# Attention beside a gated MLP on one core: head sums in four batches of five units, and the gate products moved from GpSimd to VectorE

## The chip, the cores and the metric

One core of one Trainium2 chip. The metric is device time of the whole program in microseconds (us), the median of several executions; lower is better. The unit of work on TensorE in this kernel is one 128x512 matmul, which takes 0.216 us here (groups of five start 1.079 us apart).

## The reference

A layer norm of x (2048 rows of 640), then two branches and a residual: attention with 32 heads of 20, where each row sees itself and the seven rows 2, 4, ... 14 before it; and a gated MLP of width 1536.

```python
def _A_ref(x, wqkv, wo):                       # H = 32, Dh = 20, W = 8, dil = 2
    q, k, v = ...                              # from x @ wqkv
    idx = pos[:, None] - (jnp.arange(W) * dil)[None, :]
    logits = jnp.einsum("bhsd,bhswd->bhsw", q, k[idx]) * Dh ** -0.5      # masked where idx < 0
    attn = softmax(logits)
    return jnp.einsum("bhsw,bhswd->bhsd", attn, v[idx]) @ wo

def _B_ref(x, w_gate, w_up, w_down):
    return ((x @ w_gate) * (x @ w_up)) @ w_down

xn = _layernorm(x)
return x + _A_ref(xn, A_wqkv, A_wo) + _B_ref(xn, B_w_gate, B_w_up, B_w_down)
```

## The kernel before

The rows are cut into four blocks of 512 (`j`), the 640 columns into five chunks of 128 (`c`). A small scheduler written in the kernel takes tasks as they become ready *by its own estimate of time* and writes down, once and for all, the order of instructions of each engine, the PSUM bank of every result, and the semaphores. (PSUM is the kernel's tile `PS`: every matmul row of the trace writes it. The kernel uses it as eight banks, and its scheduler gives a bank out again when the engine that reads the result is done with it. SBUF holds the kernel's other tiles.) So the order is fixed when the kernel is built; at run time an engine only waits.

Attention's weighted values are made in 20 units `u = 5 j + c`. VectorE multiplies values by weights (two instructions per unit), GpSimd adds pairs (two per unit, into a buffer `SV`), and TensorE sums the rest by a matmul against a quarter-width matrix `SEL`, four of which run side by side in four column groups (from the end of the wide work before to the next start, 8, 12 and 20 of them took 0.64, 0.85 and 1.29 us in the kernel before: 0.21 to 0.22 us more for each further four). This is the **narrow form**; gate, up and down use the whole width. Units are collected into batches:

```python
    NU = NJ * NCH
    BATCH = (1, 4, 6, 9, 11, 14, 19)          # last unit of each batch
    ...
        if u in BATCH:
            K.spawn(sums(tuple(pend)))
            pend.clear()

    def sums(us):
        ...
        def go(*bs):                           # one PSUM bank per unit
            for u, b in zip(us, bs):
                for dq in range(4):
                    o, p = PS[32 * dq:32 * dq + 32, b, :], SV[sv_of[u]][:, dq, :]
                    op("pe", ... e.matmul(o, SEL[:], p, start=True, stop=True, tile_position=(0, 32 * dq)) ...)
                sv_free.append(sv_of[u])

        def ev():                              # ScalarE empties the banks into OT
            ...
        yield Task("pe", go, r=[SV[sv_of[u]][:] for u in us], prio=9.7, banks=len(us), slack=0.7)
        yield Task("act", ev, r=[PS[:, b, :] for b in hold], prio=3)
```

The gate result is copied out of PSUM by ScalarE (`h`); the product with the up result is done by VectorE straight from PSUM, or, for up to `HP_MAX` at a time, by ScalarE (copy) and GpSimd (product):

```python
                def mul():
                    X = op("dve", lambda e: e.tensor_tensor(h, h, PS[:, hold[1], :], ALU.mult), ...)
                    K.free_bank(hold[1], X)    # the bank is free when VectorE is done
                ...
                if on_pool(j, m):
                    ...
                    yield Task("act", uev, r=[PS[:, hold[1], :]], w=[us], prio=7)
                    yield Task("pool", pmul, r=[h, us], w=[h], prio=HP_PRIO, lock=True)
                    return
                yield Task("dve", mul, r=[h, PS[:, hold[1], :]], prio=H_PRIO)
```

`lock=True` marks a VectorE instruction with two SBUF operands or a GpSimd one; two such never overlap, because the scheduler puts a semaphore between them. I call this taking turns. The down projection of 128 rows and 320 columns is 12 matmuls over `h` and 5 over `OT`, in one bank. It starts for block 0 when the 12 products and the emptying of the block's head sums stand in the engines' queues; the matmuls over `OT` come last in it.

Of the kernel before, what the change touches and what calls it, by code (L numbers as in the profile page):

```python
# [6 lines left out]
ALU = mybir.AluOpType  # L7
# [3 lines left out]
D = 640  # L11
# [4 lines left out]
NF = 12  # L16
# [5 lines left out]
TS = 128  # L22
JB = 512
# [332 lines left out]
def build_kernel(nc, A_x, A_wqkv, A_wo, B_x, B_w_gate, B_w_up, B_w_down, out):  # L356
    K = Sched(nc)
    op = K.op

    place = [16512]  # L360

    def sb(name, shape, dtype=BF16, at=None):
        n = mybir.dt.size(dtype)
        for s in shape[1:]:
            n *= s
        n = (n + 63) // 64 * 64
        if at is None:
            at = place[0]
            place[0] += n
        assert at + n <= 229344, (name, at + n)  # L370
        return K.sbuf(name, shape, dtype, at)
# [8 lines left out]
    OT = sb("OT", [128, NJ, NCH, JB])  # L380
# [9 lines left out]
    a_ra = place[0]  # L390
# [5 lines left out]
    NS = 5  # L396
    SV = [sb(f"SV{i}", [128, 4, JB], at=a_pr + i * 4096) for i in range(3)]
    SV += [sb("SV3", [128, 4, JB], at=a_qk + 33024), sb("SV4", [128, 4, JB], at=a_qk + 33024 + 4096)]
    SV += [sb("SV5", [128, 4, JB], at=a_ra + 6 * D * 2)]
    sv_free = [3, 4, 0, 1, 2]  # L400
    a_sc = place[0]
    place[0] += 8192
# [7 lines left out]
    NP = len(PV)  # L410
    PRD += [sb("PRD8", [128, 4, JB], at=a_ra + 3 * NCH * D * 2)]
    LOG = [sb(f"LOG{i}", [128, 2, W, TS]) for i in range(2)]
    HX = [sb(f"HX{i}", [128, JB], at=place[0] - 8192 + i * 1024) for i in range(8)]
    PRD += [sb("PRD9", [128, 4, JB], at=place[0])]
    HX += [sb(f"HX{8 + i}", [128, JB]) for i in range(4)]
    ATX0 = sb("ATX0", [128, 2, 2, JB])
    ATX = [ATX0, sb("ATX1", [128, 2, 2, JB])]
    PRD += [sb("PRD10", [128, 4, JB], at=place[0] - 4096), sb("PRD11", [128, 4, JB], at=place[0])]
# [3 lines left out]
    QUAD = {2: (1, 0), 3: (1, 0)}  # L422
    BY_DMA = (((0, 0), (0, 2)), ((1, 0), (1, 2)))
    a_xr = place[0]
# [4 lines left out]
    XNS = sb("XNS", [128, NXN, D], at=a_xr)  # L429
    NUX = 3  # L430
    UX = sb("UX", [128, NUX, JB])
    STATS = sb("STATS", [128, NT, 12], FP32)
    MV = sb("MV", [128, NT, 2], FP32)
    SD = sb("SD", [128, NT, 4], FP32)
    DUM = sb("DUM", [128, 16], FP32)
    TCH = sb("TCH", [128, NCH, 32])
    ZERO = sb("ZERO", [128, JB])
    EPSC = sb("EPSC", [128, 16], FP32)
    IDENT = sb("IDENT", [128, 128])
    SEL = sb("SEL", [128, 32])  # L440
# [4 lines left out]
    def ht(j, m):  # L445
        if j == 3:
            return XNT[:, m % NCH, m // NCH * JB:(m // NCH + 1) * JB]
        if j == 2:
            return OT[:, 3, m - 8, :] if m >= 8 else HX[HXM[m]][:]
        return HT[:, j, m, :]  # L450

    HXM = (0, 1, 2, 3, 8, 9, 10, 11, 4, 5, 6, 7)
    WPOS = (2, 0, 1)
    done = set()
    count = {}
# [4 lines left out]
    def bump(*k):  # L460
        count[k] = count.get(k, 0) + 1
# [4 lines left out]
    def num(n, *k):  # L466
        return lambda: count.get(k, 0) >= n
# [223 lines left out]
    def evac(parts, name):  # L691
        for o, i, n in parts:
            X = op("act", (lambda o, i: lambda e: e.activation(o, i, ACT.Copy))(o, i), r=[i], w=[o], name=name,  # L693
                   occ=0.12 + n * 0.9e-3)
        return X
# [137 lines left out]

    def products():
        rows = {j: [] for j in range(NJ)}
        holds = {}
        for at, (j, kind) in enumerate(ORDER):
            if kind == "w":
                if j not in holds:
                    yield from fetch(j, 0, holds.setdefault(j, {c: [] for c in range(4)}))  # L840
                yield from wide(j, rows[j], holds[j])
            else:
                if len(QUAD.get(j, ())) == 2 and j not in holds and (j, "w") == ORDER[at + 1]:
                    yield from fetch(j, 0, holds.setdefault(j, {c: [] for c in range(4)}))
                for r in (1, 0):
                    for c in range(NCH - 1 if r in QUAD.get(j, ()) else 0, NCH):
                        yield from narrow(j, r, c, rows[j])
            if len(rows[j]) == 10 - 3 * len(QUAD.get(j, ())):
                K.spawn(logits(j, rows[j]))
        mark("products")  # L850

    def narrow(j, r, c, slots):
# [105 lines left out]
            free.append(A)  # L958
        parts.append(q0)

    def logits(j, slots):
        hold = []
        for e in slots:
            if len(e) > 3:
                yield lambda: len(e[3]) == 2
        slots.sort(key=lambda e: -e[2])
        n1 = sum(e[2] for e in slots)

        def go(*bs):
            for i, e in enumerate(slots):  # L970
                n, s, r = e[:3]
                b, i, nt = bs[1 - r], i - (0 if r else n1), n1 if r else len(slots) - n1
                for a in range(4):
                    o = PS[32 * a:32 * a + 32, b, :].rearrange("p (q s) -> p q s", q=4)
                    x = s[:, :, a * TS:(a + 1) * TS]
                    op("pe", (lambda o, x, i, a, nt: lambda e: e.matmul(o, G[:], x, start=(i == 0), stop=(i == nt - 1),  # L976
                                                                   tile_position=(0, 32 * a)))(o, x, i, a, nt),
                       r=[G[:], x], w=[o], name=f"lg{j}_{r}_{i}_{a}", occ=0.054, lat=0.4, mode=1)
                free.append(n)
            hold.extend(bs)  # L980

        def dst(r):
            return LOG[j // 2][:, j % 2, 4 * r:4 * r + 4, :]

        def ev(r):
            b, d = hold[1 - r], dst(r)
            X = op("act", lambda e: e.activation(d, PS[:, b, :].rearrange("p (q s) -> p q s", q=4), ACT.Copy, scale=SCALE),  # L987
                   r=[PS[:, b, :]], w=[d], name=f"lgev{j}_{r}", occ=0.58)
            K.free_bank(b, X)
            if j == 0:  # L990
                for s in range(4):
                    w = 3 - s + 4 * (1 - r)
                    if w:
                        m = LOG[0][0:32, 0, 4 * r + s, 0:DIL * w]
                        op("pool", (lambda m: lambda e: e.memset(m, NEG))(m), w=[m], name=f"mask{w}", occ=0.2)  # L995

        yield Task("pe", go, r=[e[1][:] for e in slots], prio=9.5, banks=2, slack=2.0 if j in QUAD else 0.5)
        bump("lg")
        for r in (1, 0):
            yield Task("act", lambda: ev(r), r=[PS[:, hold[1 - r], :]], w=[dst(r)], prio=2)  # L1000
        bump("logits", j // 2)

    def softmax(x):
        def tt(o, a, b, f, name, occ):
# [58 lines left out]
        yield Task("sp", move, r=[L[:]], prio=4)  # L1063

    NU = NJ * NCH
    BATCH = (1, 4, 6, 9, 11, 14, 19)

    def vx_loads():
        yield have("products")
# [41 lines left out]
    def unit(u):  # L1111
# [1 line left out]
        if c == 0:  # L1113
            yield have("atx", j // 2)
        yield have("vx", u)
        if not more and count.get(("dn", 0), 0) >= 8:
            more.append(1)
            sv_free.extend(range(NS, len(SV)))
        yield lambda: len(sv_free) > 0 and (sv_free[0] in (3, 4) or count.get(("lg",), 0) >= NJ)
        sv_of[u] = sv_free.pop(0)  # L1120
        sv = SV[sv_of[u]]
# [97 lines left out]
        yield Task("act", ev, r=[PS[:, b, :] for b in hold], prio=3)  # L1219

    ucount = [0]

    def on_pool(j, m):
        return count.get(("lg",), 0) >= NJ and m < 11 and ucount[0] - count.get(("hp",), 0) < HP_MAX

    def gu(j):
# [14 lines left out]
        for m in range(NF):  # L1241
# [15 lines left out]
            def after(h=h, hold=hold, j=j, m=m):  # L1257
# [11 lines left out]
                if on_pool(j, m):  # L1269
# [16 lines left out]
                    yield room(1.15)  # L1286
                    yield Task("pool", pmul, r=[h, us], w=[h], prio=HP_PRIO, lock=True)
                    return
                yield Task("dve", mul, r=[h, PS[:, hold[1], :]], prio=H_PRIO)

            yield Task("pe", lambda b: go(0, b), prio=50, banks=1, keep=GU_KEEP, r=[WG[:]])
            K.spawn(after())
# [26 lines left out]
    def dn_piece(j, t, nb, rows, c0, c1):  # L1319
# [63 lines left out]
        yield Task("pe", down, prio=41, banks=1, keep=0 if count.get(("ot", j), 0) >= NCH else DN_KEEP, r=[WD[:], WO[:]])  # L1383
        K.spawn(tail())

    SLIP = 0.3
    N_PE_T = 4
    BN_AFTER = (4,)
# [3 lines left out]
    N_SPLIT = 2  # L1392
    FIRST = 9
    GU_KEEP = 3
    HP_MAX = 2
    ORDER = ((0, "n"), (1, "n"), (2, "n"), (3, "n"), (2, "w"), (3, "w"))
    LAST = ORDER[-1][0]
    HP_PRIO = 30
    DN_KEEP = 3
    H_PRIO = 9  # L1400
    FIN_PRIO = 8

# [76 lines left out]
```

## Time and profile before

| | kernel before |
|---|---|
| time | 267.76 us, median of 4 (267.72 to 267.81) |
| TensorE busy | 260.7 us, 98% of a span of 266.0 us |
| VectorE, GpSimd, ScalarE busy | 217.0, 154.5, 112.0 us |
| visits of head sums to the narrow form | 7 (2, 3, 2, 3, 2, 3, 5 units) |
| gate products | 38 on VectorE from PSUM, 10 on GpSimd |

How to read the lines below: a row of a timeline is start, duration, engine, line of the kernel, operation, output<-inputs, shape and count; in brackets stands idle time of the engine just ahead and what ended it. Durations on TensorE are modelled at their ends, so I reckon with **starts**: where a row of n matmuls starts, the next row should start n x 0.216 us (128x512) or n x 0.136 us (128x320) later. What is more than that is a wait, the price of a change of form, or a record that is missing from the trace (in the kernel before, 17 of TensorE's 1,764).

### The profile page before, as it was taken

What the parts mean: (1) busy time and instruction counts of PE and PEld (TensorE: products, weight loads), DVE (VectorE), ACT (ScalarE), POOL (GpSimd) and SP (SyncE); (2) the same over time, 40 slices, a digit from 0 to 9 for tenths busy, and PEclk for the clock granted to TensorE, in tenths of its full rate; (3) what the DMA queues carried; (4) which work ended last, traced back from release to release, by engine and by line L of the source; (5) the groups of instructions that cost most, each with busy time, mean ns of one, the idle gap of its engine ahead of it and who ended that gap; (6) DMA issues with size and microseconds to landing.
All of it is one profiled execution on the core that took longest, in us unless ns stands there. A gap on an engine that the chain in (4) does not pass through costs nothing.

```text
span 266.0 us, 4403 instructions
## 1 busy us (share of the span) xinstructions
PE 260.7 (98%) x1747; PEld 151.8 (57%) x1764; DVE 217.0 (82%) x249; ACT 112.0 (42%) x203; POOL 154.5 (58%) x99
## 2 busy tenths in 40 slices
PE   8999999999999999999999999999999999999996
PEld 5996965444444444444444444667466746774775
DVE  4687899999998699898699998998699979961211
ACT  3469997556622212242365426432443243116100
POOL 3000000000644996299955599999999989999000
DMA  7963689960489993831399143553885385006101
GB/s 211 372 208 78 126 149 382 385 248 1 124 147 192 241 212 75 166 76 30 73 334 201 36 112 83 133 147 80 182 181 157 85 146 112 2 0 94 32 25 53
DMA packets 39685, 37.84 MB, mean 142 GB/s; under 512 B 15824, under 2 KB 37328, under 8 KB 39632
## 3 DMA queue, kind: packets, MB, share of 16 engines
q1 hardware_dynamic: 36688, 31.35, 43.6%
q0 software_dynamic: 2736, 6.16, 13.6%
q8 instruction: 14, 0.23, 0.4%
q10 hardware_dynamic: 240, 0.05, 0.1%
q14 instruction: 7, 0.06, 0.1%
HBM read 25.07 MB, written 7.23 MB: 121 GB/s over the span
## 4 chain that ended last, share of the span: by engine, by line
PE 92%; ACT 5%; issue 1%; DVE 0%
PE PS L1253 39%; PE PS L1335 28%; PE PS L688 17%; ACT XNS L599 3%; PE PS L976 2%; PE PS L720 2%; PE PS L1204 2%; PE PS L672 2%; ACT QT L693 1%; ACT VST L693 1%; PE PS L632 1%; ACT KT L693 1%; ACT SD L574 0%; ACT HX L693 0%; DVE XNT L642 0%
## 5 line engine op out<-in xcount | busy, mean ns | idle before, releaser
L1154 POOL TENSOR_TENSOR SV<-PV 128x1024 bf16<-128x1024 f32 x40 | 95.0, 2535 | 9.6 <-DVE LOG L1033 3.3
L1149 DVE TENSOR_TENSOR PV<-VX,PS 128x1024 f32<-128x1024 bf16 (+1 forms) x54 | 91.0, 1729 | 5.4 <-POOL SV L1154 4.5
L688 PE MATMUL PS<-XNT,WQKV 128*128 128x512 bf16 (+2 forms) x384 | 60.0, 315 | 0.7 <-issue 0.5
L1253 PE MATMUL PS<-XNT,WG 128*128 128x512 bf16 x235 | 58.6, 379 | 0.3
L1253 PE MATMUL PS<-XNT,WU 128*128 128x512 bf16 x234 | 58.4, 379 | 0.4 <-ACT HX L693 0.2
L688 PEld LDWEIGHTS PS<-XNT,WQKV 128*128 128x128 bf16 x390 | 37.8, 112 | 22.1 <-ACT LOG L987 0.8
L1253 PEld LDWEIGHTS PS<-XNT,WU 128*128 128x128 bf16 x240 | 23.2, 98 | 29.0 <-issue 0.8
L1253 PEld LDWEIGHTS PS<-XNT,WG 128*128 128x128 bf16 x240 | 23.5, 98 | 27.8
L910 DVE TENSOR_TENSOR PRF<-PS,KT 128x1024 f32<-128x1024 f32 x32 | 37.8, 1216 | 0.3 <-PE PS L688 0.3
L693 ACT ACTIVATE HT<-PS 128x512 bf16<-128x512 f32 x24 | 14.3, 597 | 41.9 <-PE PS L1253 41.9
L936 POOL TENSOR_TENSOR PRF<-PRF,PRF 128x1024 f32<-128x1024 f32 x8 | 18.8, 2359 | 21.8 <-DVE LOG L1033 20.6
L1335 PE MATMUL PS<-WD,HT 128*128 128x320 bf16 x192 | 28.7, 299 | 0.0
L693 ACT ACTIVATE FB<-PS 128x320 bf16<-128x320 f32 x24 | 10.5, 438 | 41.1 <-PE PS L1335 38.4
L863 DVE TENSOR_TENSOR PRD<-QT,KT 128x2048 bf16<-128x2048 bf16 x24 | 27.3, 1217 | 0.0
L1335 PE MATMUL PS<-WO,OT 128*128 128x320 bf16 (+1 forms) x165 | 27.0, 295 | 0.0
L995 POOL MEMSET LOG<- 32x6 bf16 (+6 forms) x7 | 0.4, 95 | 44.2 <-ACT LOG L987 44.2
L1335 PEld LDWEIGHTS PS<-WD,HT 128*128 128x128 bf16 x192 | 18.6, 98 | 8.2 <-ACT FB L693 0.4
L1262 DVE TENSOR_TENSOR HT<-HT,PS 128x512 bf16<-128x512 bf16 x24 | 16.4, 685 | 8.0 <-PE PS L1253 7.9
L1335 PEld LDWEIGHTS PS<-WO,OT 128*128 128x128 bf16 x165 | 15.8, 98 | 6.2 <-issue 0.4
L954 POOL TENSOR_TENSOR PRD<-PRF,PRF 128x1024 bf16<-128x1024 f32 x8 | 18.7, 2354 | 0.9 <-DVE PRF L910 0.8
L1348 DVE TENSOR_TENSOR FB<-PS,XR 128x320 bf16<-128x320 f32 (+1 forms) x9 | 4.1, 454 | 15.3 <-PE PS L1335 15.3
L564 DVE BATCH_NORM_STATS2 STATS<-XST 128x6 f32<-128x320 bf16 x32 | 14.1, 471 | 2.4 <-DMA XST<-in_A_x_dram 2.4
(69 smaller groups left out, 238.9 us busy)
## 6 DMA issues: line engine op xcount, KB each, us to landing
VX<-v_scratch SPq DMA_DIRECT2D x80, 130.0 KB, 3.0
PRF<-PRF POOLq DMA_DIRECT2D x8, 512.0 KB, 5.2
XST<-in_A_x_dram SPq DMA_DIRECT2D x16, 160.0 KB, 5.6
v_scratch<-VST SPq DMA_DIRECT2D x4, 640.0 KB, 5.8
WG<-in_B_w_gate_dram SPq DMA_DIRECT2D x1, 1920.0 KB, 7.9
WU<-in_B_w_up_dram SPq DMA_DIRECT2D x1, 1920.0 KB, 11.9
out_dram<-in_A_x_dram SPq DMA_DIRECT2D x1, 1920.0 KB, 18.4
WD<-in_B_w_down_dram SPq DMA_DIRECT2D x1, 1920.0 KB, 8.5
```

The lines of the kernel that those rows point to most:

```text
L564: op("dve", lambda e: e.bn_stats(o, a), r=[a], w=[("st", t, i)], name=f"bn{t}_{i}", occ=0.49)
L688: op("pe", (lambda o, l, x, c, first: lambda e: e.matmul(o, l, x, start=first, stop=(c == NCH - 1)))(o, l, x, c, first), r=[l, x], w=[o], ...
L693: X = op("act", (lambda o, i: lambda e: e.activation(o, i, ACT.Copy))(o, i), r=[i], w=[o], name=name, occ=0.12 + n * 0.9e-3)
L863: op("dve", lambda e: e.tensor_tensor(s[:], qb, kv, ALU.mult), r=[q, rk], w=[s[:]], name=f"prod{j}_{r}_{c}", occ=1.15, lock=True)
L910: X = op("dve", lambda e: e.tensor_tensor(o[:], qb, kv, ALU.mult), r=[q, rk, ("qev", j, c)], w=[o[:]], name=f"prow{j}_{r}_{c}_{q0}", occ=1.17)
L936: yield Task("pool", lambda: op("pool", lambda e: e.tensor_tensor(x, x, y, ALU.add), r=[x, y] + tokens(), w=[x], name=name, occ=2.36, lock ...
L954: yield Task("pool", lambda: op("pool", lambda e: e.tensor_tensor(o, a, y, ALU.add), r=[a, y] + tokens(), w=[o], name=f"qend{j}_{r}_{q0}", ...
L1149: op("dve", lambda e: e.tensor_tensor(p, vw, a, ALU.mult), r=[vv] + rk, w=[p], name=f"pv{u}_{x}_{r0}", occ=0.09 + 1.1 * nr)
L1154: X = op("pool", lambda e: e.tensor_tensor(o, p[:, :, 0, :], p[:, :, 1, :], ALU.add), r=[p[:]] + tokens(), w=[o], name=f"pva{u}_{x}", occ= ...
L1253: op("pe", (lambda l, x, c: lambda e: e.matmul(PS[:, b, :], l, x, start=(c == 0), stop=(c == NCH - 1)))(l, x, c), r=[l, x], w=[PS[:, b, :] ...
L1262: X = op("dve", lambda e: e.tensor_tensor(h, h, PS[:, hold[1], :], ALU.mult), r=[h, PS[:, hold[1], :]], w=[h], name=f"h{m}_{j}", occ=0.65)
L1335: op("pe", (lambda l, x, i: lambda e: e.matmul(dst, l, x, start=(i == 0), stop=(i == n - 1)))(l, x, i), r=[l, x], w=[PS[:, b, :]], name=f" ...
```

## The change

Its intent: fewer visits of TensorE to the narrow form (four batches of five units), with more `SV` buffers laid over rows that are dead by then; no product on GpSimd any more; and, to keep VectorE in time, the 12 products of the third block from two SBUF operands, after ScalarE has copied the up result out of PSUM too. I call those the **fast products**.

```diff
-    BATCH = (1, 4, 6, 9, 11, 14, 19)
+    BATCH = (4, 9, 14, 19)
...
+    SV += [sb(f"SV{6 + i}", [128, 4, JB], at=a_ra + NF * JB * 2 + i * 4096) for i in range(3)]
+    SV += [sb("SV9", [128, 4, JB], at=place[0] - 4096)]
...
+    UF = [sb("UF0", [128, JB], at=a_xr + 4 * D * 2), ZERO]
...
-                yield Task("dve", mul, r=[h, PS[:, hold[1], :]], prio=H_PRIO)
+                if not fast(j, m):
+                    yield Task("dve", mul, r=[h, PS[:, hold[1], :]], prio=H_PRIO)
+                    return
+                ...
+                def fmul():
+                    op("dve", lambda e: e.tensor_tensor(h, h, us, ALU.mult), r=[h, us], w=[h], name=f"h{m}_{j}", occ=0.34, lock=True)
+                ...
+                yield Task("act", fev, r=[PS[:, hold[1], :]], w=[us], prio=7)
+                yield num(k0, "hf")
+                yield Task("dve", fmul, r=[h, us], prio=H_PRIO, lock=True)
...
+    FAST = [(2, m) for m in range(NF)]
+    JOIN = ()
-    HP_MAX = 2
+    HP_MAX = 0
-    DN_KEEP = 3
+    DN_KEEP = 5
```

Cut: the rules that say when each new buffer is free, and code that can put the logits of two blocks into one visit (`JOIN`, left empty). `DN_KEEP` is the number of banks that must stay free beside its own when a down piece is started before the head sums are emptied.

More of the change, by code (lines that the diff above doesn't have):

```diff
@@ L412, in build_kernel @@
     LOG = [sb(f"LOG{i}", [128, 2, W, TS]) for i in range(2)]
-    HX = [sb(f"HX{i}", [128, JB], at=place[0] - 8192 + i * 1024) for i in range(8)]
+    HX = [sb(f"HX{i}", [128, JB], at=place[0] - 8192 + i * 1024) for i in range(4)]
+    SV += [sb("SV9", [128, 4, JB], at=place[0] - 4096)]
     PRD += [sb("PRD9", [128, 4, JB], at=place[0])]
-    HX += [sb(f"HX{8 + i}", [128, JB]) for i in range(4)]
+    HX += [sb(f"HX{4 + i}", [128, JB]) for i in range(4)]
     ATX0 = sb("ATX0", [128, 2, 2, JB])
@@ L431, in build_kernel @@
     UX = sb("UX", [128, NUX, JB])
+    NUF = 2
     STATS = sb("STATS", [128, NT, 12], FP32)
@@ L448, in ht @@
         if j == 2:
-            return OT[:, 3, m - 8, :] if m >= 8 else HX[HXM[m]][:]
+            return OT[:, 3, m - 8, :] if m >= 8 else HX[m][:]
         return HT[:, j, m, :]
-    HXM = (0, 1, 2, 3, 8, 9, 10, 11, 4, 5, 6, 7)
     WPOS = (2, 0, 1)
@@ L835, in products @@
         rows = {j: [] for j in range(NJ)}
+        joined = []
         holds = {}
@@ L848, in products @@
             if len(rows[j]) == 10 - 3 * len(QUAD.get(j, ())):
-                K.spawn(logits(j, rows[j]))
+                if j in JOIN:
+                    joined.append((j, rows[j]))
+                    if len(joined) == len(JOIN):
+                        K.spawn(logits(*joined))
+                else:
+                    K.spawn(logits((j, rows[j])))
         mark("products")
@@ L959, in close, with logits @@
         parts.append(q0)
-    def logits(j, slots):
+    def logits(*blocks):
         hold = []
-        for e in slots:
-            if len(e) > 3:
-                yield lambda: len(e[3]) == 2
-        slots.sort(key=lambda e: -e[2])
-        n1 = sum(e[2] for e in slots)
-        def go(*bs):
-            for i, e in enumerate(slots):
-                n, s, r = e[:3]
-                b, i, nt = bs[1 - r], i - (0 if r else n1), n1 if r else len(slots) - n1
-                for a in range(4):
-                    o = PS[32 * a:32 * a + 32, b, :].rearrange("p (q s) -> p q s", q=4)
-                    x = s[:, :, a * TS:(a + 1) * TS]
-                    op("pe", (lambda o, x, i, a, nt: lambda e: e.matmul(o, G[:], x, start=(i == 0), stop=(i == nt - 1),
-                                                                   tile_position=(0, 32 * a)))(o, x, i, a, nt),
-                       r=[G[:], x], w=[o], name=f"lg{j}_{r}_{i}_{a}", occ=0.054, lat=0.4, mode=1)
-                free.append(n)
+        for _, slots in blocks:
+            for e in slots:
+                if len(e) > 3:
+                    yield (lambda p: lambda: len(p) == 2)(e[3])
+            slots.sort(key=lambda e: -e[2])
+        def go(*bs):
+            for k, (j, slots) in enumerate(blocks):
+                n1 = sum(e[2] for e in slots)
+                for i, e in enumerate(slots):
+                    n, s, r = e[:3]
+                    b, i, nt = bs[2 * k + 1 - r], i - (0 if r else n1), n1 if r else len(slots) - n1
+                    for a in range(4):
+                        o = PS[32 * a:32 * a + 32, b, :].rearrange("p (q s) -> p q s", q=4)
+                        x = s[:, :, a * TS:(a + 1) * TS]
+                        op("pe", (lambda o, x, i, a, nt: lambda e: e.matmul(o, G[:], x, start=(i == 0), stop=(i == nt - 1),
+                                                                           tile_position=(0, 32 * a)))(o, x, i, a, nt),
+                           r=[G[:], x], w=[o], name=f"lg{j}_{r}_{i}_{a}", occ=0.054, lat=0.4, mode=1)
+                    free.append(n)
@@ L980, in go, with dst, ev @@
             hold.extend(bs)
-        def dst(r):
+        def dst(j, r):
             return LOG[j // 2][:, j % 2, 4 * r:4 * r + 4, :]
-        def ev(r):
-            b, d = hold[1 - r], dst(r)
+        def ev(k, j, r):
+            b, d = hold[2 * k + 1 - r], dst(j, r)
             X = op("act", lambda e: e.activation(d, PS[:, b, :].rearrange("p (q s) -> p q s", q=4), ACT.Copy, scale=SCALE),
@@ L995, in ev @@
                         op("pool", (lambda m: lambda e: e.memset(m, NEG))(m), w=[m], name=f"mask{w}", occ=0.2)
-        yield Task("pe", go, r=[e[1][:] for e in slots], prio=9.5, banks=2, slack=2.0 if j in QUAD else 0.5)
-        bump("lg")
-        for r in (1, 0):
-            yield Task("act", lambda: ev(r), r=[PS[:, hold[1 - r], :]], w=[dst(r)], prio=2)
-        bump("logits", j // 2)
+        yield Task("pe", go, r=[e[1][:] for _, slots in blocks for e in slots], prio=9.5, banks=2 * len(blocks),
+                   slack=2.0 if blocks[-1][0] in QUAD else 0.5)
+        for _ in blocks:
+            bump("lg")
+        for k, (j, _) in enumerate(blocks):
+            for r in (1, 0):
+                yield Task("act", (lambda k, j, r: lambda: ev(k, j, r))(k, j, r), r=[PS[:, hold[2 * k + 1 - r], :]], w=[dst(j, r)], prio=2)
+            bump("logits", j // 2)
     def softmax(x):
@@ L1115, in unit @@
         yield have("vx", u)
-        if not more and count.get(("dn", 0), 0) >= 8:
-            more.append(1)
-            sv_free.extend(range(NS, len(SV)))
+        for k, (ok, n) in enumerate(((("atx", 1) in done, (9,)), (count.get(("dn", 0), 0) >= 8, (5,)),
+                                     (count.get(("dn", 1), 0) >= 8, (6, 7, 8)))):
+            if ok and k not in more:
+                more.append(k)
+                sv_free.extend(n)
         yield lambda: len(sv_free) > 0 and (sv_free[0] in (3, 4) or count.get(("lg",), 0) >= NJ)
@@ L1221, in build_kernel, with fast @@
     ucount = [0]
+    fcount = [0]
+    def fast(j, m):
+        return (j, m) in FAST
     def on_pool(j, m):
@@ L1288, in after, with fev @@
                     return
-                yield Task("dve", mul, r=[h, PS[:, hold[1], :]], prio=H_PRIO)
+                if not fast(j, m):
+                    yield Task("dve", mul, r=[h, PS[:, hold[1], :]], prio=H_PRIO)
+                    return
+                k0 = fcount[0]
+                fcount[0] += 1
+                us = UF[k0 % NUF][:]
+                def fev():
+                    K.free_bank(hold[1], evac([(us, PS[:, hold[1], :], JB)], f"uev{m}_{j}"))
+                def fmul():
+                    op("dve", lambda e: e.tensor_tensor(h, h, us, ALU.mult), r=[h, us], w=[h], name=f"h{m}_{j}", occ=0.34, lock=True)
+                    bump("hf")
+                    bump("h", j)
+                yield num(k0 - NUF + 1, "hf")
+                yield Task("act", fev, r=[PS[:, hold[1], :]], w=[us], prio=7)
+                yield num(k0, "hf")
+                yield Task("dve", fmul, r=[h, us], prio=H_PRIO, lock=True)
             yield Task("pe", lambda b: go(0, b), prio=50, banks=1, keep=GU_KEEP, r=[WG[:]])
```

## The prediction

The sum came to 267.78 - 0.63 (three visits) + 0.2 (the wait of step 5) = 267.35 us, told as 267.3, and the prices in it, 0.21 us a visit and 685 or 424 ns a product, are read from the trace of the kernel before. That a batch of five takes five banks stands in `sums` above.

> **What bounds the kernel now.** I read the page first, then the chain that ended last in order of time, then the timeline of TensorE, then the groups by form, then the timelines of GpSimd and VectorE. The page says who is full and who ends last:
>
> ```profile
> PE 260.7 (98%) x1747; PEld 151.8 (57%) x1764; DVE 217.0 (82%) x249; ACT 112.0 (42%) x203; POOL 154.5 (58%) x99
> ...
> PE 92%; ACT 5%; issue 1%; DVE 0%
> ```
>
> TensorE is busy for 98% of the span and makes 92% of the chain. Its busy time is a modelled one, so 98% alone proves little; what counts is the spacing of its starts. The timeline of TensorE around the head sums (the SV<-PV additions end in them; they use a quarter-width stationary operand, 128*32):
>
> ```profile
> 164.91 1.24 PE L1253 MATMUL PS<-XNT,WG 128*128 128x512 bf16 x5
> 166.08 0.83 PE L1204 MATMUL PS<-SV,SEL 128*32 128x512 bf16 x12
> 166.84 1.25 PE L1253 MATMUL PS<-XNT,WU 128*128 128x512 bf16 x5
> ...
> 176.49 0.84 PE L1335 MATMUL PS<-WO,OT 128*128 128x320 bf16 x5
> 177.26 0.62 PE L1204 MATMUL PS<-SV,SEL 128*32 128x512 bf16 x8
> 177.81 1.80 PE L1335 MATMUL PS<-WD,HT 128*128 128x320 bf16 x12
> ...
> 242.58 1.24 PE L1253 MATMUL PS<-XNT,WU 128*128 128x512 bf16 x5
> 243.75 1.26 PE L1204 MATMUL PS<-SV,SEL 128*32 128x512 bf16 x20
> 244.95 3.43 PE L1335 MATMUL PS<-WD,XNT 128*128 128x320 bf16 x24
> ```
>
> Groups of five gate or up matmuls start 1.079 us apart all along, 0.216 us each; a down piece of 12+5 starts every 2.308 us, 0.136 us each. No start from 35.6 us to 263.6 us is late by anything but a missing record, a change to or from the quarter-width form, or about 0.2 us of issue. So from there to the end TensorE is the bound, and only work taken from its own stream can shorten the kernel; a faster GpSimd or VectorE is worth nothing in itself, and can only cost if it comes too late.
>
> The three rows of x12, x8 and x20 give the price of a change of form. Next start minus (last wide start + its 5 matmuls): 166.84 - (164.91 + 1.079) = 0.85 for x12; 177.81 - (176.49 + 0.679) = 0.64 for x8; 244.95 - (242.58 + 1.079) = 1.29 for x20. Four narrow matmuls run beside each other in the time of one (the page's 112 logit matmuls do the same), so the work in them is 3, 2 and 5 times 0.216: 0.65, 0.43, 1.08. What is left is **0.21 us per batch**, three times over, whatever its size.
>
> GpSimd and the products it shares with VectorE:
>
> ```profile
> L1154 POOL TENSOR_TENSOR SV<-PV 128x1024 bf16<-128x1024 f32 x40 | 95.0, 2535 | 9.6 <-DVE LOG L1033 3.3 <-DVE SM L1006 3.2 <-DVE LOG L1019 3.1
> L1262 DVE TENSOR_TENSOR HT<-HT,PS 128x512 bf16<-128x512 bf16 x24 | 16.4, 685 | 8.0 <-PE PS L1253 7.9
> L1279 POOL TENSOR_TENSOR XNT<-XNT,UX 128x512 bf16<-128x512 bf16 x6 | 7.8, 1394 | 0.0
> L1279 POOL TENSOR_TENSOR HX<-HX,UX 128x512 bf16<-128x512 bf16 x3 | 3.5, 1158 | 0.0
> L1006 DVE TENSOR_TENSOR M<-M 128x512 bf16<-128x512 bf16 x2 | 0.8, 424 | 0.1
> ```
>
> The reader should see that the 40 additions are a chain on GpSimd (start to start 2.31 us in its long rows), that it waited for VectorE's softmax rows of two SBUF operands (LOG, SM), and that the same 128x512 product takes 685 ns on VectorE from PSUM, 1.16 us or more on GpSimd, and 424 ns where both operands are in SBUF.
>
> [...]
>
> **The change part by part.** The order of TensorE's instructions is the same up to the second block's gate matmuls (about 141 us). Read after that from the order of instructions, with durations of before.
>
> 1. Batches 2, 3, 2, 3, 2, 3, 5 become 5, 5, 5, 5. The 80 narrow matmuls stay. Three visits fewer: 3 x 0.21 = -0.63 us, all on the path.
> 2. The flags for joined logits are empty: the code for it changes nothing.
> 3. Ten products leave GpSimd (three HX, six XNT, one OT): 7.8 + 3.5 + 1.2 = 12.5 us there (the OT row of the groups has 1.2). VectorE had 38, all from PSUM; it now has 36 from PSUM and the 12 of the third block from SBUF: 36 x 0.685 + 12 x 0.424 - 38 x 0.685 = +3.7 us. ScalarE evacuates 12 up results in place of 10: +1.2 us. All beside TensorE: 0 on the path, if nothing comes late.
> 4. The 12 products take turns with GpSimd: an addition stands between two of them, so the additions of units 2 to 4 (132 to 163 us) run at VectorE's step. This decides whether the first batch is ready. By hand from the order of both engines: subtraction of the maximum ends at 138.6, addition of unit 1 at 141.0, exponent, sums and unit 2's second product to 146.7, normalisation to 148.6, then addition and product in turn: unit 2 at 151.2, unit 3 at 154.0 and 156.9, unit 4's four half products to 160.0, its additions at 161.2 and 163.5. TensorE comes to the batch at 166.08 - 0.65 (the first batch gone) - 1.08 (one up group later) = 164.35, and to its fifth unit 0.9 us after that. Spare: about 1.7 us.
> 5. Right behind it the first down matmul waits for the bank of the third product of the last block. VectorE has then 0.4 us (last fast product, held to 163.5 by the addition), 1.15 us and 0.69 us to do: 165.7. TensorE is there at 164.25 + 1.29 = 165.54. Cost +0.2 us, give or take the chain's error.
> 6. Later batches: GpSimd goes on at 2.31 us an addition, ten per batch: 189.1 with a store's issue, against TensorE at 190.7; 213.1 against 217.0; 237.7 (it waits once for VectorE, 1.5 us) against 240.0. New buffers (SV5 to SV9) are free before they are asked for. Cost 0. The last batch now has three groups behind it, so the last product is covered by the 12 down matmuls (1.6 us against 0.9). Cost 0.
>
> Sum: 267.78 - 0.63 + 0.2 = 267.35; I say 267.3.
>
> **The rivals.** First, the turns between VectorE and GpSimd make the first batch late: item 4 has 1.7 us of spare on a chain of some 30 us, and the queue of item 5 moves with it. For it: the chain passes exp and the reciprocal on ScalarE, and GpSimd's three waits of 3.1, 3.2 and 3.3 us show that the softmax stops it. Against it: 12.5 us less work on GpSimd. If the chain is 2 us longer than I worked out, the kernel is at 269. Second, five banks at once starve the matmuls that follow: ScalarE needs 5 x 0.52 = 2.6 us to empty them, against 2.3 us for each down piece that asks for the next bank; the x20 batch of before was followed by down pieces without a gap, so I give this 0 to 0.3 us at each of three batches: up to 268. Third, GpSimd was the hidden bound and freeing it pays: the additions end 6 us earlier. Against it: no late start in TensorE's timeline, so nothing is there to win; this would be 265 or less, and I hold it for out.
>
> **Range and chances.** The gain is bounded by 0.63 us (267.15) plus noise of 0.1; the losses are one-sided. 266.9 to 268.0 should hold it 8 times in 10. 2% is 5.4 us: faster needs a gap that the timeline doesn't have, slower needs 6 us of stalls, and the worst rival makes 2. Faster 0.01, within 2% 0.98, slower 0.01.
>
> **What would show it.** Right: four groups of x20 narrow matmuls, each 1.29 us from the end of the wide group before to the next start; products of two SBUF operands at 0.42 us; GpSimd with 89 or so instructions, some 142 us busy and 0 products; TensorE starts as regular as before. Step 5 would be a gap of about 0.2 us before the first down matmul near 165.6 us, released by VectorE. Wrong: a gap in TensorE before a narrow group released by GpSimd (first rival), gaps between down pieces released by ScalarE (second), or a narrow batch that costs other than 0.21 us.

## The result, and the profile after

The changed kernel took **267.72 us** (median of 4, 267.65 to 268.06) against 267.76 us for the kernel before. The ratio is 1.0001, 95% interval 0.9983 to 1.0018: the same. A ratio here is the mean time of one kernel's fast runs over that of the other's of the same rounds, so not quite the ratio of the medians. The time was predicted to within half a microsecond, so the work that follows is about the parts, which are larger than their sum.

The page of the changed kernel, busy times and the engines' shares of the chain that ended last:

```profile
PE 261.3 (98%) x1764; PEld 152.4 (57%) x1764; DVE 219.5 (83%) x259; ACT 113.1 (43%) x205; POOL 143.5 (54%) x89
...
PE 97%; DVE 1%; DMA 1%; issue 0%; ACT 0%
```

GpSimd gave up 11 us and VectorE took 2.5 us; TensorE is as full as before. VectorE's share of the chain goes from 0% to 1%; 0.3% is one product that the next lines show, the rest lies in the first 9 us and in the last row. The timeline of TensorE in the changed kernel, first and second batch:

```profile
163.28 1.24 PE L1274 MATMUL PS<-XNT,WU 128*128 128x512 bf16 x5
164.45 1.26 PE L1220 MATMUL PS<-SV,SEL 128*32 128x512 bf16 x20
166.12 3.43 PE L1374 MATMUL PS<-WD,HT 128*128 128x320 bf16 x24 [0.41 <-DVE XNT L1283]
...
190.00 1.24 PE L1274 MATMUL PS<-XNT,WU 128*128 128x512 bf16 x5
191.18 1.26 PE L1220 MATMUL PS<-SV,SEL 128*32 128x512 bf16 x20
192.37 3.43 PE L1374 MATMUL PS<-WD,HT 128*128 128x320 bf16 x24
```

The second batch costs what it should: 192.37 - (190.00 + 1.079) = 1.29 us, of which 1.08 is work and **0.21** the change of form. The third and fourth give 1.29 too. The first costs 166.12 - (163.28 + 1.079) = 1.76, that is **0.47 us too much**, and the bracket says what ended the wait: a VectorE product of the last block. It is the only idle time that TensorE's timeline of the changed kernel marks after the first 9 us. The chain of the changed kernel goes through the same place (start, length, engine):

```profile
164.52 0.82 PE PS L1220 x12
165.33 0.05 issue
165.39 0.69 DVE XNT L1283
166.08 0.04 issue
166.12 18.65 PE PS L1374 x136
```

And these are VectorE's queue there and GpSimd's last two additions before it:

```profile
163.91 0.42 DVE L1321 TENSOR_TENSOR OT<-OT,ZERO 128x512 bf16<-128x512 bf16 x1 [0.20 <-POOL SV L1170]
164.25 1.22 DVE L1165 TENSOR_TENSOR PV<-VX,PS 128x1024 f32<-128x1024 bf16 x1
165.39 0.68 DVE L1283 TENSOR_TENSOR XNT<-XNT,PS 128x512 bf16<-128x512 bf16 x1
```

```profile
159.21 4.67 POOL L1170 TENSOR_TENSOR SV<-PV 128x1024 bf16<-128x1024 f32 x2 [2.01 <-DVE PV L1165]
```

The last fast product (424 ns, in `OT`) waits 0.20 us for GpSimd's last addition of unit 4 (over at 163.88); a weighting of 1.2 us and then the third product of the last block stand behind it. That product frees the bank which the scheduler gave to the first down matmul. When the kernel is built, the scheduler's own estimate has this product end at 164.48 us, 0.42 us before it lets the down matmul start (164.90); in the trace it ends at 166.07, 0.42 us after TensorE could have started (166.12 - 0.47 = 165.65).

**A yardstick finer than the time.** Two traces of one and the same kernel may be 0.6 us apart before the changed part begins. The timeline of TensorE at the first logits of one version of the kernel (the one called pair_between below), in two runs:

```profile
45.05 2.34 PE L987 MATMUL PS<-PRD,G 128*32 128x512 bf16 x40
```

```profile
45.64 2.34 PE L987 MATMUL PS<-PRD,G 128*32 128x512 bf16 x40
```

The 0.59 us arise among the first transposes, between 8 and 15 us. So beside the time I give for every run the **stretch** from the start of this row to the start of VectorE's last result row. Before: 263.67 - 45.15 = 218.52 us. After: 263.60 - 45.25 = 218.35 us.

### The profile page after: what moved, and what is told of

It reads as the page before. It is cut to its first block, busy times and chain, and to the rows that moved or that the text cites. A ratio compares the mean times of both kernels' runs of the same rounds, so it can differ in the third digit from the quotient of the medians.

```text
span 265.9 us, 4425 instructions
## 1 busy us (share of the span) xinstructions
PE 261.3 (98%) x1764; PEld 152.4 (57%) x1764; DVE 219.5 (83%) x259; ACT 113.1 (43%) x205; POOL 143.5 (54%) x89
## 3 DMA queue, kind: packets, MB, share of 16 engines
q0 software_dynamic: 2736, 6.16, 13.6%
## 4 chain that ended last, share of the span: by engine, by line
PE 97%; DVE 1%; DMA 1%; issue 0%; ACT 0%
PE PS L1274 39%; PE PS L1374 28%; PE PS L691 23%; PE PS L987 2%; PE PS L723 2%; PE PS L1220 2%; DMA XST<-in_A_x_dram 1%; PE PS L635 1%; DVE STATS L567 0%; DVE XNT L1283 0%; PE PS L675 0%; DVE XNS L596 0%; DVE XNT L645 0%; DVE FB L1387 0%; ACT SD L577 0%
## 5 line engine op out<-in xcount | busy, mean ns | idle before, releaser
L1170 POOL TENSOR_TENSOR SV<-PV 128x1024 bf16<-128x1024 f32 x40 | 94.1, 2526 | 14.9 <-DVE LOG L1033 4.0
L691 PE MATMUL PS<-XNT,WQKV 128*128 128x512 bf16 (+2 forms) x390 | 60.9, 316 | 0.0
L1274 PE MATMUL PS<-XNT,WU 128*128 128x512 bf16 x240 | 59.7, 379 | 0.0
L1274 PE MATMUL PS<-XNT,WG 128*128 128x512 bf16 x240 | 59.6, 379 | 0.0
L1283 DVE TENSOR_TENSOR XNT<-XNT,PS 128x512 bf16<-128x512 bf16 x12 | 8.2, 684 | 9.4 <-PE PS L1274 9.4
```

What stands on the lines that cost most here:

```text
L691: op("pe", (lambda o, l, x, c, first: lambda e: e.matmul(o, l, x, start=first, stop=(c == NCH - 1)))(o, l, x, c, first), r=[l, x], w=[o], ...
L1170: X = op("pool", lambda e: e.tensor_tensor(o, p[:, :, 0, :], p[:, :, 1, :], ALU.add), r=[p[:]] + tokens(), w=[o], name=f"pva{u}_{x}", occ= ...
L1274: op("pe", (lambda l, x, c: lambda e: e.matmul(PS[:, b, :], l, x, start=(c == 0), stop=(c == NCH - 1)))(l, x, c), r=[l, x], w=[PS[:, b, :] ...
```

## The experiments

Theory one: the time is TensorE's stream. A visit to the narrow form costs 0.21 us whatever its size, so three fewer give 0.63 us; a wait of 0.47 us at the first down matmul takes most of it back, because a bank comes late out of VectorE's queue, which the fast products tie to GpSimd. Theory two, in several forms: visits cost nothing, or the loss lies elsewhere (ScalarE emptying five banks at once; GpSimd; or VectorE simply too full).

If theory one holds, each run's stretch should be 218.52 + 0.21 x (visits - 7) + the waits read off its own timeline of TensorE:

| run | visits | waits seen, us | sum | stretch | median time, us | ratio to before, 95% interval |
|---|---|---|---|---|---|---|
| before | 7 | 0 | (base) | 218.52 | 267.76 | |
| after_again | 4 | 0.47 | 218.36 | 218.34 | 267.71 | 0.9992 [0.998, 1.0005] |
| old_batches | 7 | 0 | 218.52 | 218.52 | 267.86 | 1.0000 [0.9988, 1.0013] |
| eleven_batches | 11 | 0 | 219.36 | 219.41 | 268.75 | 1.0035 [1.0022, 1.0047] |
| pair_between | 4 | 0.12 | 218.01 | 217.98 | 267.20 | 0.9978 [0.9964, 0.9992] |
| pair_repeat | 4 | 0.09 | 217.98 | 217.95 | 267.20 | 0.9979 [0.9966, 0.9992] |
| batches_alone | 4 | 0.19 | 218.08 | 218.06 | 267.50 | 0.9990 [0.9976, 1.0004] |
| no_fast | 4 | 1.33 | 219.22 | 219.19 | 268.56 | 1.0027 [1.0015, 1.0040] |
| unlocked | 4 | 1.03 | 218.92 | 218.90 | 268.25 | 1.0014 [1.0002, 1.0027] |
| third_block_pool | 4 | 0 | 217.89 | 217.87 | 267.18 | 0.9978 [0.9966, 0.9989] |
| last_from_psum | 4 | 0 | 217.89 | 217.86 | 267.05 | 0.9978 [0.9966, 0.9989] |

(after_again stands for the changed kernel. The eleventh run, join23, is not a matter of tenths and is told below.) Sum and stretch agree within 0.05 us in all ten. As the waits are read off the same traces, this shows that the price of a visit is constant and that nothing else is lost; what causes a wait must come from the edits. The runs, one by one; each edit is against the changed kernel.

**after_again**: the changed kernel unaltered.

> The changed kernel unaltered, as the mark for the other runs on the same chip. Both theories: 267.7 us, within 0.15 of the kernel before, with one wait of about 0.45 us of TensorE before the first down matmul, ended by VectorE's third product of the last block, and four batches of head sums at 1.29 us each.

Measured 267.71 us, the wait 0.47 us again. As expected by both theories.

**old_batches and eleven_batches**: more visits.

```diff
-    BATCH = (4, 9, 14, 19)
+    BATCH = (1, 4, 6, 9, 11, 14, 19)                     # old_batches
+    BATCH = (1, 3, 4, 6, 8, 9, 11, 13, 14, 16, 19)       # eleven_batches
```

> The changed kernel with the seven old batches again, the fast products kept. Theory one (each visit to the narrow form costs 0.21 us, and the wait at the first down matmul took 0.47 us of the 0.63 us saved): three visits more, +0.63; but one up group now stands between the small batch and the first down matmul, so the wait goes, -0.47: 267.85 us, 0.1 above the kernel before. Theory two (visits cost nothing or less than measured, the change gave nothing to lose): 267.25 us, half a microsecond below the kernel before, since only the wait goes.

> The changed kernel with eleven small batches of one to three units in place of four of five. Theory one: seven visits more, 7 x 0.21 = +1.47 us, and no wait at the first down matmul (-0.47): 268.7 us, and each visit shows 0.21 us beyond its work whatever its size, one unit too. Theory two (visits cost nothing): 267.25 us. A cost that goes with the number of units would give 267.25 too, as there are 20 units in every case.

Measured 267.86 and 268.75 us, where theory one said 267.85 and 268.7, and theory two 267.25 for both. The timeline of TensorE with eleven batches shows the smallest visit, one unit:

```profile
163.35 1.24 PE L1274 MATMUL PS<-XNT,WG 128*128 128x512 bf16 x5
164.53 0.40 PE L1220 MATMUL PS<-SV,SEL 128*32 128x512 bf16 x4
164.86 1.25 PE L1274 MATMUL PS<-XNT,WU 128*128 128x512 bf16 x5
```

164.86 - (163.35 + 1.079) = 0.43 us, less 0.216 of work: 0.21 again, as for 2, 3 and 5 units. It can be split: the narrow row starts 0.10 us after the wide one is through, and the next wide row 0.11 us after the narrow one is through. So the cost goes with the visits, not with the units; the rival is out. That old_batches is at the time of before with VectorE's fast products, the new buffers and `DN_KEEP` in it also shows that those, in themselves, cost TensorE nothing.

**pair_between**: one gate group more before the first batch.

```diff
         if us[-1] >= 3 * NCH:
             yield num(8, "dn", 2)
+        if us[0] == 0:
+            yield num(3, "h", NJ - 1)
```

> The changed kernel, but its first batch waits until the third product of the last block is in VectorE's queue, so that TensorE does the next gate group (1.08 us) before the batch and comes to the first down matmul so much later. Theory one: the wait of 0.47 us is covered, nothing else moves: 267.25 us, half a microsecond below the kernel before. Theory two (five banks taken at once starve the down pieces; the wait only moves to the next bank, emptied by ScalarE): 267.7 us, with a wait of 0.3 to 0.5 us ended by ScalarE near 167 us.

> The version with one gate group before the first batch, once more on another chip, to see whether its gain holds. Theory one: 0.5 to 0.6 us below the kernel before, no wait of TensorE over 0.15 us after the first batch. If the first reading was chance: within 0.2 us of the kernel before.

Measured 267.20 us twice, on two chips; the intervals of the ratio lie wholly below 1. The timeline of TensorE:

```profile
164.16 1.24 PE L1276 MATMUL PS<-XNT,WG 128*128 128x512 bf16 x5
165.33 1.26 PE L1222 MATMUL PS<-SV,SEL 128*32 128x512 bf16 x20
166.52 3.44 PE L1376 MATMUL PS<-WD,HT 128*128 128x320 bf16 x24
```

166.52 - (164.16 + 1.079) = 1.28 us: the wait is gone and none comes in its place at the next bank, so ScalarE's emptying of five banks is not what held it. About 0.1 us shows after the second batch. The edit moved more than the time, however: the schedule that this version builds gives the bank of VectorE's third product to the fifth head sum (which starts at 165.99 us, 0.11 us after the product's end), and the first down matmul takes a bank that ScalarE empties. So this run does not tell a later TensorE from another bank.

**batches_alone**: the four batches, with the products where they were before.

```diff
-    FAST = [(2, m) for m in range(NF)]
+    FAST = []
-    HP_MAX = 0
+    HP_MAX = 2
```

> The four batches of five alone: no product from two SBUF operands, up to two at a time on GpSimd as in the kernel before. Theory one (the visits give 0.63 us; the wait at the first down matmul is made by the last fast product, tied to GpSimd's last addition, in VectorE's queue): the third product of the last block and the bank that the first down matmul takes are not behind a fast product here, so no wait: 267.15 us, 0.63 below the kernel before. Theory two (the large first batch itself makes the loss, through its five banks that ScalarE empties, or because GpSimd's additions are not ready with its products still on it): a wait of 0.4 us or more at or just before the first down matmul ended by ScalarE or GpSimd, 267.6 us.

Measured 267.50 us: a miss for both theories, the ratio's interval doesn't exclude 1. There is no wait at the first batch (165.62 - 163.25 - 1.079 = 1.29), which is theory one's, but one at the last, which neither had. The timelines of TensorE and of GpSimd there:

```profile
244.36 3.63 PE L1374 MATMUL PS<-WD,XNT 128*128 128x320 bf16 x24
247.82 1.52 PE L1374 MATMUL PS<-WO,OT 128*128 128x320 bf16 x10
```

```profile
242.83 3.03 POOL L1300 TENSOR_TENSOR XNT<-XNT,UX 128x512 bf16<-128x512 bf16 x2
```

24 down matmuls take 3.27 us from start to start elsewhere (3.27 at the last batch of the kernel before) and 3.46 here. GpSimd's last two products end at 245.86, and the eleventh matmul of the first piece, which would start at 244.36 + 10 x 0.136 = 245.72, reads the last of them. So 0.19 us of the 0.63 are lost to GpSimd's products; this is what the second part of the change is good for.

**no_fast**: all 48 products on VectorE from PSUM.

```diff
-    FAST = [(2, m) for m in range(NF)]
+    FAST = []
```

> Four batches, no product on GpSimd, and all 48 products on VectorE from PSUM (none from two SBUF operands). VectorE has 12 x (0.685 - 0.424) = 3.1 us more to do and the schedule puts the first batch four groups (4.3 us) later. Theory one: without the turns between fast products and additions nothing ties VectorE's queue to GpSimd, the fifth product of the last block ends near 169.2 us and TensorE asks for its bank near 170: no wait, 267.15 to 267.25 us. Theory two (the fast products are what keeps VectorE in time): VectorE is late, the first down matmul waits 0.5 us or more, 267.7 us or above.

Measured 268.56 us, ratio 1.0027, slower than before. Theory one's expectation for the first batch held (170.36 - 168.00 - 1.079 = 1.28 us, no wait); its sum failed, because VectorE's later queue held back GpSimd's additions (the last ends at 244.88 us, in the changed kernel at 238.78) and so moved the last batch, which neither theory had in view. It now lies inside a down piece, with no gate group behind it. The timelines of TensorE and ScalarE:

```profile
245.22 1.26 PE L1220 MATMUL PS<-SV,SEL 128*32 128x512 bf16 x20
246.42 0.70 PE L1374 MATMUL PS<-WO,OT 128*128 128x320 bf16 x2
247.31 0.31 PE L1374 MATMUL PS<-WO,OT 128*128 128x320 bf16 x1 [0.18 <-ACT OT L1229]
...
248.43 1.79 PE L1374 MATMUL PS<-WD,XNT 128*128 128x320 bf16 x12
```

```profile
245.68 2.56 ACT L1229 ACTIVATE OT<-PS 128x512 bf16<-128x512 f32 x5 [2.46 <-PE PS L1220]
```

The five matmuls over `OT` run at the pace at which ScalarE empties the five banks, 0.5 us each: 248.43 - (246.42 + 5 x 0.136) = 1.33 us lost. This is the rival of the prediction about emptying five banks, at a place where the fixed order puts nothing between the sums and the matmuls that read them.

**unlocked**: a fast product and an addition may overlap.

```diff
-  op("dve", lambda e: e.tensor_tensor(h, h, us, ALU.mult), r=[h, us], w=[h], name=f"h{m}_{j}", occ=0.34, lock=True)
+  op("dve", lambda e: e.tensor_tensor(h, h, us, ALU.mult), r=[h, us], w=[h], name=f"h{m}_{j}", occ=0.34)
-  yield Task("dve", fmul, r=[h, us], prio=H_PRIO, lock=True)
+  yield Task("dve", fmul, r=[h, us], prio=H_PRIO)
```

> The changed kernel, but a fast product and an addition of GpSimd may run at the same time: no turns between them. TensorE's order is the same. Theory one (the enforced turns hold the last fast product and with it the queue): its waits go, the third product of the last block ends a microsecond or more earlier, no wait at the first down matmul: 267.25 us; fast products still 0.42 us. Theory two (the two engines hinder each other in the chip, so that the turns only make visible what would be lost anyway): fast products of 0.6 us or more, or additions longer than 2.53 us where they meet, and the wait of 0.4 us stays: 267.7 us.

Theory one was wrong here and theory two right, to more than its figure: 268.25 us. Two of the fast products in `OT` among the groups by form, in the changed kernel and here, the same two in VectorE's timeline of this run, and GpSimd's timeline at the first of them:

```profile
L1321 DVE TENSOR_TENSOR OT<-OT,ZERO 128x512 bf16<-128x512 bf16 x2 | 0.9, 426 | 0.4 <-POOL SV L1170 0.4
```

```profile
L1321 DVE TENSOR_TENSOR OT<-OT,ZERO 128x512 bf16<-128x512 bf16 x2 | 3.1, 1550 | 0.0
```

```profile
154.84 1.45 DVE L1321 TENSOR_TENSOR OT<-OT,ZERO 128x512 bf16<-128x512 bf16 x1
...
159.94 1.65 DVE L1321 TENSOR_TENSOR OT<-OT,ZERO 128x512 bf16<-128x512 bf16 x1
```

```profile
151.00 5.01 POOL L1170 TENSOR_TENSOR SV<-PV 128x1024 bf16<-128x1024 f32 x2 [1.52 <-DVE LOG L1047]
```

The same two products take 426 ns in the changed kernel and 1,550 here. The first ends at 156.29 us, 0.28 us after the additions beside it (156.01), as if it had been held until they were through; no semaphore asks for it. The second ends at 161.59; the additions beside it start at 158.97, and the first of them, at the 2.36 us of one alone, would be over at 161.33, 0.26 us earlier. Among the other ten products one more is long, by the groups' means (four in `HX` of 466 ns here, 424 in the changed kernel, so about 0.6 us for it); the groups of the rest average 421 and 413 ns. The additions lose too: the two pairs shown by GpSimd's timeline at 151.00 and 158.97 us take 5.01 and 4.85 us, where the pair at 159.21 in the changed kernel takes 4.67, though the mean over all 40 hardly moves (2,537 against 2,526 ns). So the turns are not a needless rule of the scheduler. TensorE's wait at the first down matmul grew from 0.47 to 1.03 us and the time by 0.5: the cost follows the wait.

**join23**: the logits of the last two blocks in one visit.

```diff
-    JOIN = ()
+    JOIN = (2, 3)
```

> The changed kernel with the logits of the last two blocks in one visit to the narrow form instead of two (the code of the change that its empty flags leave dead). Theory one: one visit less, -0.21 us; the first batch comes later against GpSimd and the first down matmul takes a bank that ScalarE empties, so VectorE's wait goes as well: 267.7 - 0.21 - 0.47 = 267.05 us. Theory two (visits cost nothing): 267.25 us at best; or, as the logits of the third block come later, the softmax and with it all the later additions slip and new waits ended by GpSimd appear: 268 us or more.

Measured 281.48 us (4 runs, 281.05 to 281.88), far off theory one; theory two had the kind of it ("new waits ended by GpSimd"), neither the place nor the size. The timeline of TensorE:

```profile
123.67 1.04 PE L987 MATMUL PS<-PRD,G 128*32 128x512 bf16 x8 [5.52 <-POOL PRD L963]
130.71 0.62 PE L987 MATMUL PS<-PRD,G 128*32 128x512 bf16 x4 [5.99 <-POOL PRD L963]
131.26 2.31 PE L1274 MATMUL PS<-XNT,WG 128*128 128x512 bf16 x5
133.37 2.34 PE L1274 MATMUL PS<-XNT,WU 128*128 128x512 bf16 x5
```

TensorE stood before the joined logits until GpSimd had summed the last block's products, 11.5 us in two stretches, and from the work between the two on it ran at half its pace. The 8 narrow matmuls at 123.67 us took 1.04 us (8 of them 0.62 in the kernel before), and the first two groups of five took 2.11 and 2.13 us from start to start in place of 1.08, 0.42 us per matmul. The page's granted clock agrees: tenths of 7, 5 and 7 in the slices of 7 us from 119 to 140 us, 9 or more in all others. The third group took 1.29 us and the fourth 1.08, so the full pace was back 4.2 to 5.5 us after the first group had started (131.26). Saving one visit is worth 0.21 us; the run with it took 13.6 us more than the kernel before, over sixty times that.

**third_block_pool**: no fast product, GpSimd's products in the third block alone.

```diff
-    return count.get(("lg",), 0) >= NJ and m < 11 and ucount[0] - count.get(("hp",), 0) < HP_MAX
+    return count.get(("lg",), 0) >= NJ and m < 11 and j < 3 and ucount[0] - count.get(("hp",), 0) < HP_MAX
-    FAST = [(2, m) for m in range(NF)]
+    FAST = []
-    HP_MAX = 0
+    HP_MAX = 2
```

> Four batches of five, no product from two SBUF operands, and products on GpSimd for the third block alone (four of them), so that none is near the last batch. With all eleven GpSimd products the four batches lost about 0.2 us behind the last batch, where the last GpSimd product ended late. Theory one: that wait goes too and the whole 0.63 us of the three visits is left: 267.15 to 267.25 us, 0.6 below the kernel before. Theory two (fast products are needed, VectorE becomes late when it takes 44 products from PSUM): a wait ended by VectorE or ScalarE at the first or the last batch as in the version without products on either, 267.6 us or more.

**last_from_psum**: the last product of the third block from PSUM.

```diff
-    FAST = [(2, m) for m in range(NF)]
+    FAST = [(2, m) for m in range(NF - 1)]
```

> The changed kernel, but the last product of the third block is taken from PSUM (0.685 us in place of 0.424), so that it needs no turn with GpSimd's addition and goes ahead of it in VectorE's queue; the schedule then gives the first down matmul the bank that the first head sum of the batch leaves. Theory one (that one turn and the queue behind it make the wait): no wait, 267.25 us, 0.5 below the kernel before. Theory two (VectorE as a whole is late near 165 us, and 0.26 us more work there makes it later): a wait of 0.4 to 0.7 us ended by VectorE, or by ScalarE's emptying of the sums, stays within the first two down pieces: 267.7 to 268.0 us.

Both times came out as theory one said: 267.18 and 267.05 us, no wait over 0.1 us, and stretches of 217.87 and 217.86 us, the whole of three visits below before. The timeline of TensorE in third_block_pool:

```profile
163.06 1.24 PE L1274 MATMUL PS<-XNT,WU 128*128 128x512 bf16 x5
164.23 1.26 PE L1220 MATMUL PS<-SV,SEL 128*32 128x512 bf16 x20
165.43 3.43 PE L1374 MATMUL PS<-WD,HT 128*128 128x320 bf16 x24
```

165.43 - (163.06 + 1.079) = 1.29 us, no wait. third_block_pool shows that the twelve fast products are not needed: four products on GpSimd, far from the last batch, do as well. As evidence for the cause both are weaker than they look. The timelines of TensorE and VectorE in last_from_psum:

```profile
165.45 1.80 PE L1374 MATMUL PS<-WD,HT 128*128 128x320 bf16 x12
```

```profile
165.16 0.68 DVE L1283 TENSOR_TENSOR XNT<-XNT,PS 128x512 bf16<-128x512 bf16 x1
```

The third product of the last block still ends at 165.84 us, after TensorE's start at 165.45. The wait is gone because the scheduler, with another estimate, gave the first down matmul another bank, not because VectorE came earlier by enough. In third_block_pool it is the same: the product ends at 165.80 us, TensorE has started at 165.43.

The traces say more about theory one than these runs were made for. Counted from the start of the stretch, VectorE's third product of the last block ends at 120.82 us in the changed kernel, 120.83 in pair_between, 120.79 in last_from_psum (no turn just before it), 120.77 in third_block_pool and 120.77 in no_fast (no fast product at all). So taking the turns away together with the fast products doesn't bring it forward, and the part of theory one that blames the tie to GpSimd is not shown; the 0.20 us of idle time at the last turn is real, but without it the queue is no shorter. Why the ends agree so well no run tells. What is shown is that the wait is for that bank. By the traces' records the first down matmul waits in the changed kernel and in unlocked for VectorE's semaphore, and is late. In pair_between, third_block_pool, last_from_psum and batches_alone it waits for ScalarE's, for another bank, and is not late. No run keeps the bank and moves TensorE alone, or the reverse.

## Why the prediction was right or wrong

- **What bounds the kernel.** Right. Every version's stretch is TensorE's work plus the visits plus the waits seen, to 0.05 us, whether VectorE was busy for 216.5 or 222.4 us and GpSimd for 143.5 or 155.5 (join23, told apart, is not in that table).
- **Step 1, three visits, -0.63 us.** Right, and now shown by adding visits as well as by taking them away.
- **Step 2, the empty flags.** Right that they do nothing; the code behind them, switched on for the last two blocks, costs 13.6 us against the kernel before.
- **Step 3, moved products cost TensorE nothing.** Right. VectorE's busy time grew by 2.5 us, not 3.7: the products come out as reckoned (36 of 685 and 12 of 424 ns, 1.6 times as fast from two SBUF operands as from PSUM; the copy of the up result ahead of each takes ScalarE about 0.6 us), and the durations of all rows do add up to 3.9 us more. But the records of neighbouring rows overlap, by 1.4 us more in all with ten rows more, and the busy time counts that once. GpSimd's 11.0 us in place of 12.5 has the same reason: its rows overlap by 2.4 us less.
- **Step 4, the first batch is ready.** Right: the narrow row starts 0.10 us after the wide one is through, as at every visit. The chain worked out by hand slipped by 0.1 us at unit 2 (151.27 for 151.2), 0.2 and 0.3 at unit 3 (154.24, 157.20) and 0.4 at unit 4 (161.57, 163.88). The batch had the spare for it; step 5 had not.
- **Step 5, +0.2 us at the first down matmul.** Right in place, engine and path, too small in size: 0.47 us. The term that was off is the end of VectorE's queue, 166.07 us where the working by hand had 165.7. From the start of the last fast product the queue took 2.15 us (2.24 reckoned); what was late is the fast product itself, 163.91 for 163.5, because GpSimd's last addition of unit 4 ended at 163.88 for 163.5. TensorE was there at 165.65 (0.1 later than reckoned, as the whole run was at 45 us). The step named the right bank; the experiments show that the wait hangs on that choice.
- **Step 6, later batches cost nothing.** Right for the changed kernel. Two experiments show how near it was: with GpSimd's products kept 0.19 us, without fast products 1.33 us, both at the last batch.
- **The sum.** -0.63 + 0.47 = -0.16 us on the stretch (measured -0.17), where -0.43 was predicted; the time of 267.7 lies 0.4 above the 267.3 told, inside the range. That the range held says little about the steps: 266.9 to 268.0 also holds a change that does nothing, and the 0.43 us foretold is smaller than the 0.6 us by which two traces of one kernel can differ.
- **The rivals.** The first (turns make the batch late) did not stop the batch; the same chain, 0.4 us late, is step 5's overrun. The second (five banks starve what follows) was not there; it shows only in no_fast, where the order puts nothing between the sums and their readers. The third (GpSimd as hidden bound) is out.

So the change did what it was meant to do on TensorE, and gave three quarters of it back at one spot. Three small edits (pair_between, third_block_pool, last_from_psum) keep the whole gain, about 0.6 us or 0.2%: the kernel before is beaten by ratios whose intervals lie below 1. Against the changed kernel there is no interval; the stretches are shorter by 0.37 to 0.49 us.

## What to carry to other kernels

When one engine is full, price each removable overhead by starts (next start minus last start minus work), and then look at the first consumer behind each regrouped piece: a larger group comes later by its own length and takes its inputs and banks in one go, so the slack there must be reckoned afresh. In a kernel whose order is fixed when it is built, compare the scheduler's estimate with the trace at the place of a wait: here it took a bank to be free 0.4 us before TensorE came, the trace has it free 0.4 us after, and each version that handed out another bank lost nothing there. Where effects are smaller than the scatter of runs, compare stretches within a trace, from a common point to the end, and check that they add up.
